# Two batches sharing the arrival of float64 weights, with clamp and gelu moved to ScalarE

## The chip, the cores and the metric

One core of one Trainium2 chip. Times are device microseconds (us) of one execution. A time given for a kernel is the median of its runs. The record marks each run as fast or slow by its granted clock and time. Engines are named as the profile has them: PE is TensorE (PEld its weight loads), DVE is VectorE, ACT is ScalarE, POOL is GpSimd, SP is SyncE, which issues the loads.

## The reference

Eight batches of 8 heads. Tokens read from 32 state vectors a head and the states read from the tokens; both results go through one gated layer whose weights are float64.

```python
B, H, S, Ns, D = 8, 8, 512, 32, 64
scores = scale * np.matmul(x, state.transpose(0, 1, 3, 2))     # softmax over states -> a
xread = np.matmul(a, state)
scores2 = scale * np.matmul(state, x.transpose(0, 1, 3, 2))    # softmax over tokens -> a2
sread = np.matmul(a2, x)
x = np.concatenate([xread, sread], axis=2)                     # ... to (B*(S+Ns), H*D)
h = x @ w_in                                                   # w_in 512 x 2048, float64
g = h * (1.0 / (1.0 + np.exp(-1.702 * h)))
return (g @ w_out).astype(np.float32)                          # w_out 2048 x 512, float64
```

## The kernel before

The weights arrive as pairs of 32-bit words, in 32 pieces of 128x512 numbers (512 KB each): 16 of `w_in`, then 16 of `w_out`. Each piece is rounded to float32 by integer and float instructions. Three raw buffers hold what has landed and isn't rounded yet.

```python
def load_weight(key, src):                     # w_in: two halves of 64 partitions; w_out: one load
    raw[key] = wpool.tile([P, 2 * FC], I32, tag="raw", ..., bufs=3)
    for i in range(src.shape[0]):
        nc.sync.dma_start(raw[key][n * i : n * (i + 1)], src[i])

def round_weight(key, dst):
    ...                                                                           # hi, lo: the words of each number
    sc = wpool.tile([P, FC], I32, tag="sc", ...)
    nc.vector.tensor_scalar(sc, hi, 0x7FF00000, None, ALU.bitwise_and)            # mask of the exponent
    nc.gpsimd.tensor_scalar(sc, sc, most, least, ALU.min, ALU.max)                # clamp
    nc.gpsimd.tensor_scalar(sc, sc, -least, 8.0, ALU.add, ALU.mult)
    nc.vector.scalar_tensor_tensor(sc, hi, -0x80000000, sc, ALU.bitwise_and, ALU.bitwise_or)
    fr = wpool.tile([P, FC], I32, tag="fr", ...)
    nc.vector.tensor_scalar(fr, hi, 0xFFFFF, 0x100000, ALU.bitwise_and, ALU.bitwise_or)
    nc.vector.scalar_tensor_tensor(dst, lo, 2.0**-32, fr, ALU.mult, ALU.add)
    nc.vector.scalar_tensor_tensor(dst, dst, 2.0**-20, sc.bitcast(FP32), ALU.mult, ALU.mult)
```

A batch's work around PE: transposes, scores and softmax; `eT`, the transposed token weights, and `sr`, the states' read with them (`srT` is its copy); `M` = states times `w_in` (four chunks); 16 "ups" (two matmuls to `h`, then gelu to `g`); 64 "downs" of `g` and `w_out` into `o`. In the kernel before, batch 0 alone does this while the weights arrive. DVE's order is left to a scheduler; the other engines run in the order of the program.

```python
def up(key, f, ntok, lhs, rhs):
    ...                                                          # matmuls into hps
    nc.scalar.activation(out=e, in_=hps, func=AF.Sigmoid, scale=1.702)
    nc.vector.tensor_tensor(out=gt, in0=hps, in1=e, op=ALU.mult)

load(0)
for c in range(NFC):                     # NFC = 4
    load_w_in(c); round_w_in(c)
    if c == 0: ...                       # all of batch 0's attention
    att_M(0, c)
load(1)
for b in range(B):
    for f in range(NF):                  # NF = 16
        if b == 0: load_w_out(f); round_w_out(f)
        up(b, f, ...)
    ...                                  # 16 groups of downs; batch b+1's attention in between
...                                      # last: ups and downs of all the states' tokens
```

## Time and profile before

| | before |
|---|---|
| median of the first three runs | 931.3 us (930.19 to 931.96) |
| PE without a gap from | 146.2 us |
| one batch from there on | 94.80 us |
| one `w_out` piece on DVE | 3.48 us |
| DVE's waits for raw weights | none |

The lines that carry this stand in the prediction. A busy row has one digit for each fortieth of the span: the busy share in tenths. A line of the timeline reads: start, duration, engine, program line, operation, out<-in, shapes, and in brackets how long the engine had been idle and what released it.

### The profile page before, as it was taken

The page shows a single profiled execution, that of the slowest core. Times are in us where ns is not written, and L with a number is a line of the kernel's source. Part 1 is how long each engine was busy: PE and PEld are TensorE (multiplying, and loading weights), DVE is VectorE, ACT ScalarE, POOL GpSimd, SP SyncE. Part 2 cuts the span into 40 slices and gives each one's busy share as a digit, 9 for nine tenths or more (in the row PEclk, how much of TensorE's full clock was granted, in tenths as well). Part 3 has the DMA queues.
Part 4 walks back from the last instruction along what each step waited for, and adds up shares of the span by engine and source line. Part 5 has one row for each costly group of instructions (what it writes and reads, how often), then busy time and mean ns, then how long its engine had stood idle before and what let it go on. Part 6 is the DMA issues. An engine that isn't in the chain of part 4 may idle for free.

```text
span 930.2 us, 7058 instructions
## 1 busy us (share of the span) xinstructions
PE 850.7 (91%) x2824; PEld 384.4 (41%) x2824; DVE 320.3 (34%) x544; ACT 169.7 (18%) x282; POOL 73.5 (8%) x104
## 2 busy tenths in 40 slices
PE   3545568999999999999999999999999999999995
PEld 1301224345444544354435443544354435444762
DVE  5786896413232223322232314231523141300110
ACT  1001111213121322122212221221222021300110
POOL 2242442000000000000000000000000000000000
PEclk8555799999999999999999999999999999999998
DMA  6256343002000200020002000200000000000001
GB/s 161 62 141 161 113 136 97 24 11 57 3 23 12 57 4 23 12 56 4 23 12 57 3 12 24 56 1 11 24 12 0 12 23 11 1 11 23 11 1 23
DMA packets 43968, 35.06 MB, mean 38 GB/s; under 512 B 37664, under 2 KB 37664, under 8 KB 43936
## 3 DMA queue, kind: packets, MB, share of 16 engines
q1 hardware_dynamic: 40832, 25.70, 10.7%
q0 software_dynamic: 3104, 8.92, 2.5%
q8 instruction: 22, 0.36, 0.2%
q14 instruction: 10, 0.08, 0.0%
HBM read 25.69 MB, written 8.91 MB: 37 GB/s over the span
## 4 chain that ended last, share of the span: by engine, by line
issue 67%; PE 18%; DVE 9%; POOL 4%; SPq 0%; DMA 0%; ACT 0%; POOLq 0%
PE o L300 11%; PE h L284 4%; POOL out_dram L306 2%; PE M L179 1%; PE sr L248 1%; DVE sc_i L133 1%; POOL sc_i L132 1%; DVE w_out L138 1%; DVE fr_o L136 1%; DVE w_out L137 1%; POOL sc_i L131 1%; DVE sc_o L133 1%; DVE w_in L138 1%; DVE g L288 1%; PE xT L169 1%
## 5 line engine op out<-in xcount | busy, mean ns | idle before, releaser
L300 PE MATMUL o<-w_out,g 128*128 128x512 f32 x1024 | 457.8, 596 | 0.0
L300 PEld LDWEIGHTS o<-w_out,g 128*128 128x128 f32 x1024 | 187.8, 190 | 236.1 <-issue 236.1
L284 PE MATMUL h<-aT,M 128*128 128x512 f32 x512 | 229.3, 606 | 21.4 <-DVE g L288 21.4
L284 PEld LDWEIGHTS h<-aT,M 128*128 128x128 f32 x512 | 92.9, 193 | 153.1 <-DVE g L288 83.4
L288 DVE TENSOR_TENSOR g<-h,e 128x512 f32<-128x512 f32 x128 | 88.4, 690 | 124.8 <-ACT e L286 124.8
L286 ACT ACTIVATE e<-h 128x512 f32<-128x512 f32 x128 | 76.4, 597 | 187.0 <-PE h L284 187.0
L179 PE MATMUL M<-w_in,stT 64*32 64x512 f32 x512 | 55.5, 658 | 26.0 <-DVE w_in L138 25.9
L306 POOL DMA_DIRECT2D out_dram<-osb x32 | 17.5, 547 | 697.7 <-ACT osb L305 697.7
L305 ACT COPY osb<-o 128x512 f32<-128x512 f32 x32 | 18.7, 586 | 192.4 <-PE o L300 192.4
L231 DVE COPY M<-M 128x512 f32<-128x512 f32 x32 | 21.8, 682 | 58.1 <-PE M L179 58.1
L231 ACT COPY M<-M 128x512 f32<-128x512 f32 x32 | 18.6, 582 | 112.6 <-PE M L179 112.6
L171 DVE COPY xT<-xT 128x512 f32<-128x512 f32 x16 | 11.1, 692 | 77.4 <-PE xT L169 77.4
L191 DVE TENSOR_REDUCE mx<-s 128x1 f32<-128x512 f32 x16 | 10.4, 687 | 79.1 <-PE s L179 79.1
L179 PEld LDWEIGHTS M<-w_in,stT 64*32 64x32 f32 x512 | 7.6, 108 | 68.1 <-issue 38.2
L248 PEld LDWEIGHTS sr<-eT,xn 128*128 128x128 f32 x256 | 33.0, 209 | 4.9 <-issue 3.3
L248 PE MATMUL sr<-eT,xn 128*128 128x64 f32 x256 | 32.9, 292 | 1.2 <-DVE eT L241 1.2
L288 DVE TENSOR_TENSOR g_sr<-h_sr,e_sr 128x256 f32<-128x256 f32 x16 | 6.8, 425 | 75.3 <-ACT e_sr L286 75.3
L257 DVE COPY srT<-sr 64x128 f32<-64x128 f32 x16 | 4.6, 289 | 73.0 <-PE sr L248 72.9
L171 ACT COPY xT<-xT 128x512 f32<-128x512 f32 x16 | 9.4, 586 | 109.6 <-PE xT L169 109.6
L284 PE MATMUL h_sr<-srT,w_in 128*128 128x256 f32 x128 | 27.8, 379 | 0.0
L300 PE MATMUL o_sr<-w_out,g_sr 128*128 128x512 f32 x64 | 27.6, 592 | 0.0
L241 DVE COPY eT<-eT 128x512 f32<-128x512 f32 x16 | 11.0, 690 | 45.5 <-PE eT L240 45.5
(52 smaller groups left out, 401.4 us busy)
## 6 DMA issues: line engine op xcount, KB each, us to landing
xn<-in_x_dram SPq DMA_DIRECT2D x64, 128.0 KB, 3.1
raw_i<-in_moe_w_in_dram SPq DMA_DIRECT2D x32, 256.0 KB, 4.2
raw_o<-in_moe_w_out_dram SPq DMA_DIRECT2D x16, 512.0 KB, 3.3
out_dram<-osb POOLq DMA_DIRECT2D x32, 256.0 KB, 2.3
stn<-in_state_dram SPq DMA_DIRECT2D x8, 64.0 KB, 2.0
out_dram<-osb_sr POOLq DMA_DIRECT2D x2, 256.0 KB, 7.1
```

Source lines behind the costliest of these rows:

```text
L133: nc.vector.scalar_tensor_tensor(sc, hi, -0x80000000, sc, ALU.bitwise_and, ALU.bitwise_or)
L138: nc.vector.scalar_tensor_tensor(dst, dst, 2.0**-20, sc.bitcast(FP32), ALU.mult, ALU.mult)
L171: (nc.scalar.copy if j % 2 else nc.vector.tensor_copy)(dst, ps.rearrange("p c q -> p (c q)"))
L179: nc.tensor.matmul(ps[g][st], A[b]["stT"][rows, st], rhs(rows, j), start=True, stop=True)
L231: (nc.scalar.copy if g else nc.vector.tensor_copy)(a["M"][:, g, FC * c : FC * (c + 1)], ps[g])
L248: nc.tensor.matmul(ps[:, j], x_heads(b, c, j), a["eT"][:, :, c, Ns * j : Ns * (j + 1)], start=(c == 0), stop=(c == SCH - 1),)
L284: nc.tensor.matmul(hps, lhs[i], rhs[i], start=(i == 0), stop=(i == n - 1))
L286: nc.scalar.activation(out=e, in_=hps, func=AF.Sigmoid, scale=1.702)
L288: nc.vector.tensor_tensor(out=gt, in0=hps, in1=e, op=ALU.mult)
L300: nc.tensor.matmul(ops, G[key][f][:, P * r : P * (r + 1)], w_out[f], start=(f == 0), stop=(f == NF - 1))
L305: nc.scalar.copy(osb, ops)
L306: nc.gpsimd.dma_start(dst, osb)
```

## The change

The intent: let batch 1's first half run on PE too while the weights arrive, so that less is left afterwards; relieve DVE of the product and of GpSimd; end the run on a plain output tile. DVE's order is now fixed by the program as well. The core of the diff:

```diff
-    ctx.enter_context(tc.manual_schedule(engines={ET.PE, ET.Activation, ET.Pool, ET.SP}))
+    ctx.enter_context(tc.manual_schedule())
@@ rounding in two parts, a and b
+    def round_a(i):
+        ...
         nc.vector.tensor_scalar(sc, hi, 0x7FF00000, None, ALU.bitwise_and)
-        nc.gpsimd.tensor_scalar(sc, sc, most, least, ALU.min, ALU.max)
-        nc.gpsimd.tensor_scalar(sc, sc, -least, 8.0, ALU.add, ALU.mult)
+        nc.scalar.activation(out=sc.bitcast(FP32), in_=sc, func=AF.Relu, bias=edge[0], scale=-8.0)
+        nc.scalar.activation(out=sc, in_=sc.bitcast(FP32), func=AF.Relu, bias=edge[1], scale=-1.0)
+    def round_b(i): ...                      # the other four DVE instructions
+    AHEAD = 2
+    def round_next(n):
+        for _ in range(n):
+            ...                              # stop behind the last piece
+            while done["a"] < min(done["b"] + 1 + AHEAD, len(PIECES)):
+                round_a(done["a"]); done["a"] += 1
+            round_b(done["b"]); done["b"] += 1
+            nxt = done["b"] + 2
+            if nxt < len(PIECES): load_weight(nxt)           # raw: bufs=3, as before
@@ gelu
-        nc.scalar.activation(out=e, in_=hps, func=AF.Sigmoid, scale=1.702)
-        nc.vector.tensor_tensor(out=gt, in0=hps, in1=e, op=ALU.mult)
+        nc.scalar.activation(out=gt, in_=hps, func=AF.Gelu_apprx_sigmoid)
@@ order of the first stage (batches 0 and 1 by chunks of M and four ups)
+    chunk(0, 0, True)                        # True: one piece is rounded after each up
+    ...                                      # batch 1's softmax
+    chunk(0, 1, True)
+    for g in range(NG): att_eT(1, g)
+    att_sread(1)
+    chunk(1, 0, False)
+    chunk(1, 1, True)
+    chunk(0, 2, True)
+    chunk(0, 3, True)
+    load_state(2); load_x(2)
+    for f in range(NF):
+        ...                                  # downs of batch 0 by rows of w_out, batch 1's other ups
+        round_next(1)
@@ the last batch
+        if not ahead: ...                    # states' ups and downs go ahead of batch 7's
```

The copies from PSUM of batches 0 and 1 all go to ScalarE, and the tile pools are resized (attention has two PSUM buffers instead of four, the downs four instead of two).

## The prediction

> **What bounds the kernel now.** I read the page first (clock and busy rows), then busy time by stretch, the chain of waits from 85 us on, the DMA issues, the timeline of the rounding stage and of the end.
>
> The busy rows say where the time is lost:
>
> ```profile
> PE   3545568999999999999999999999999999999995
> PEclk8555799999999999999999999999999999999998
> 0.00:146.22 146.22, 76.86 (x202) 27.67 (x203) 113.55 (x195) 17.65 (x28) 51.47 (x67) 0.70 0.48 133
> 146.22:931.00 784.78, 773.81 (x2624) 356.75 (x2622) 206.76 (x350) 152.09 (x254) 22.00 (x38) 0.99 0.07 20
> 290.58:385.38 94.80, 94.80 (x330) 42.30 (x329) 27.59 (x47) 20.26 (x34) 2.16 (x4) 1.00 0.08 23
> ```
>
> (columns of the last three: stretch, length, busy us and count on PE, weight loads, DVE, ACT, POOL, then clock, DMA share, GB/s). Two regimes. From 146 us the tensor engine has no gap, and a batch takes 94.80 us, so nothing but fewer matmuls or less time before that point shortens the run. Before 146 us the float64 weights arrive and are rounded to float32 piece by piece (32 pieces of 512 KB), and PE does little at a lowered clock.
>
> The chain of waits shows who paces that stage:
>
> ```profile
> 139.51 0.75 DVE fr_o L136
> 140.26 0.60 DVE g L288
> 140.85 0.60 DVE sc_o L133
> 141.46 0.60 DVE w_out L137
> 142.06 0.34 DVE sc_o L130
> 142.39 0.60 DVE w_out L138
> 142.99 0.75 DVE fr_o L136
> ```
>
> DVE is back to back, one piece in 142.99 - 139.51 = 3.48 us: five rounding instructions plus the gelu product (L288). Loads are not on this chain. Their sizes and times:
>
> ```profile
> raw_i<-in_moe_w_in_dram SPq DMA_DIRECT2D x32, 256.0 KB, 4.2
> raw_o<-in_moe_w_out_dram SPq DMA_DIRECT2D x16, 512.0 KB, 3.3
> out_dram<-osb POOLq DMA_DIRECT2D x32, 256.0 KB, 2.3
> out_dram<-osb_sr POOLq DMA_DIRECT2D x2, 256.0 KB, 7.1
> ```
>
> The last figure is us from issue to landing. They hide because a load issued when piece n is used up is first read about two pieces (7 us) later.
>
> The end: the states' output closes the run.
>
> ```profile
> 920.07 0.59 ACT L305 COPY osb_sr<-o_sr 128x512 f32<-128x512 f32 x1 [13.15 <-PE o_sr L300]
> 920.95 0.72 POOL L306 DMA_DIRECT2D out_dram<-osb_sr  x1 [13.01 <-ACT osb_sr L305]
> ```
>
> PE ends at 920.03; 920.95 + 7.1 = 928.05, and the span ends 2.1 us later.
>
> **What the Trainium skill says.** "DMA: Bandwidth & Descriptors", section "Anatomy of one DMA — SWDGE (gpsimd) path", gives a transfer a nearly constant cost of about 2 us whatever its size, most of it the receipt of the last write. The trace agrees in kind: 512 KB land in 3.3 us, so a load waited for at once cannot be cheap. "SBUF — State Buffer", section "Who interferes with whom", says that GpSimd and a DVE instruction that needs the shared port pair block each other. Before shows it: the L136 instruction takes 0.42 us alone and 0.83 us beside GpSimd, L137 0.68 and up to 1.09. "ScalarE: Activation LUTs", section "What ACT_TABLE_LOAD costs", puts a load of the tables at about 1.28 us, the same for every set; the trace has 1283 ns. "TensorE: Matmul & The Clock Gate", section "Part 1: The HAM clock gate (the "warmup" mystery)", has the array at half clock after idle windows; the clock row shows 5 tenths where PE waits.
>
> **The change part by part.**
>
> 1. Gelu as one function: takes 128 L288 products (690 ns each, 88 us) off DVE. After 146 us PE is full, so nothing is gained there. In the rounding stage it takes 0.60 us of 3.48 off each w_out piece.
>
> 2. Clamp on ScalarE: 64 GpSimd instructions go, 64 Relu activations of about 0.69 us come (the Exp with a pointer bias on 128x512 took 683 ns). DVE's slowdown beside GpSimd ends. A piece is then 0.34 + 0.34 + 0.60 + 0.60 + 0.60 = 2.5 us of DVE. If DVE alone paced it, 32 pieces would take 80 us plus two softmaxes of 10 us.
>
> 3. But the order changes. The changed order was read off the built program: the first instruction (mask of the exponent) of piece n+3 stands directly behind the last of piece n, while the load of n+3 goes into the buffer of piece n (three buffers) and waits for piece n's fourth instruction. Looking ahead two pieces with three buffers leaves no time for the load. So each step is a closed loop: mask to end of fourth instruction 0.34 + 0.34 + 0.60 + 0.68 = 1.96 us; issue 0.02; landing 3.3 us for w_out, and for w_in two halves, the second issued 0.6 us after the first and landing 3.7 us later, 4.3; start of DVE 0.05. Steps: 5.33 us (w_out), 6.33 us (w_in), against 3.5 to 3.6 now.
>
> 4. Two batches share the arrival, so PE has more to do meanwhile. Pieces that gate it, by that loop:
> - x of batch 0 and raw pieces 0 to 2 share the queue; mask of piece 2 at about 13.8 us, the x transposes' copies on ScalarE stand behind its Relus, scores end about 19.6, batch 0's softmax is done with pieces 0 and 1 rounded at 33.7.
> - pieces 2 to 7: piece 2 used up at 35.7, 3 at 42.1, then 6.33 each: piece 7 at 67.4.
> - batch 1's softmax, about 10.6 us: to 78.6. Piece 8 at 80.6, then 6.33 each: piece 13 at 112.2.
> - piece 14 needs its Relu, which stands on ScalarE behind batch 1's eT and srT copies, its M copies and five gelus; those wait for PE at half clock (sr took 7.1 us there, an up pair of matmuls 3.4 instead of 1.72). From 100 us: copies 1.2, sr 7.1, srT 0.7, M and copies 3.1, four ups 9, second M and copies 2.3, one up and its gelu 2.3: about 126. Piece 14 at 128.7, 15 at 134.1.
> - w_out, 5.33 each: piece 23 at 176.7; the mask of piece 26 at 180.1. Batch 2's x (1 MB) is queued next to that load: +1.5.
> - Batch 1's third M chunk is copied on ScalarE behind the Relus of piece 26: 1.8 + 1.2 us later, 184.5. From there PE does not wait: pieces 24 to 31 run ahead of the eight matmuls that each w_out row needs.
>
> Work of PE done by then, at full clock: attention of two batches 2 x 7.3, seven M chunks 7.2, 24 ups of 1.72 = 41.3, eight down matmuls of 0.86 = 6.9: 70 us. The whole is 8 x 94.8 + 27.5 + 27.5 = 813.4 (check: 813.4 less the 38.9 done by 146.22 is 774.5, and the trace has 920.03 - 146.22 = 773.8). Left: 743.5. With 1.5 us for the clock to come up: PE ends at 184.5 + 1.5 + 743.5 = 929.5.
>
> 5. States' tokens ahead of the last batch: the last output is a plain tile, 2.3 us to landing instead of 7.1. Tail 0.6 + 0.3 + 2.3 + 2.1 = 5.3 us instead of 10.2: gain 4.8.
>
> Sum: 929.5 + 5.3 = 934.8 by this working. The terms I padded (half clock through all of batch 1's chunk, the contention of batch 2's x) rather err high, so I say 932: the sharing gains 31 us of PE work, the slower arrival costs 40, the tail gives back 5.
>
> **Rivals.** (a) The loads don't bind: DVE paces at 2.5 us a piece, all pieces rounded near 110 us, PE full from about 85. PE left then about 765: 860 us or so, 7% faster. For it: every instruction cost of the new step is lower. Against: the order and the wait of the load are fixed in the program, and DVE takes its instructions in order. (b) ScalarE as the bound in the shared stage: per step a gelu 0.6 and two Relus 1.4 = 2.0 us, below 5.3, so no, except where a Relu stands behind PE work (piece 14, counted). If other Relus are caught so, another 10 us: 945. (c) The steady stage gets a new wait, from two attention buffers in PSUM instead of four, and the fourth M chunk inside the ups. Copies take 0.6 to 0.7 us and four down matmuls (3.4 us) lie between users, so I expect none; 1 us a batch would make 7 us. (d) Landing is shorter when only one piece is in flight: w_out already had one in flight in before and took 3.3, so little; 0.5 us a step would give 11 us: 921.
>
> **Range and chances.** The loop has 20 or so load steps on the path; 0.3 us each is 6 us, the ScalarE hold-up of piece 14 is uncertain by 6, the start by 3, the rest by 4: together 10 us, widened for an error of structure: 914 to 948. Faster by over 2% means under 912.7 and needs the loads to be half hidden: 0.14. Slower means over 950: 0.08. Within 2%: 0.78.
>
> **What would show it.** Right: DVE waits for the raw loads nearly every piece, about 2.8 us for w_out and 3.7 for w_in, some 90 us in all; masks of successive w_out pieces 5.3 us apart; PE full only from about 185 us with batches of 94.8 after; no idle on POOL's account; span end about 5 us after the last matmul. Wrong: w_out pieces at 2.5 to 3.5 us, PE full before 150 us (then rival a), or gaps in PE after 200 us (rival c).

## More of the kernel before

One more view is needed later, PE's waits in the first 240 us of the kernel before (engine, line, what it waited for: us in total, times, longest):

```profile
PE M L179 <- DVE w_in L138: 25.9, 11, 4.5
PE h L284 <- DVE g L288: 21.4, 10, 9.3
```

PE waits for rounded `w_in` pieces, and its ups wait for the gelu product, which DVE does between the rounding of `w_out`.

## The result, and the profile after

The changed kernel took 946.51 us (946.0 to 948.57, 4 runs) against 931.19 us (930.19 to 931.96, 4 runs) of the kernel before: ratio 1.0169, 95% interval 1.0151 to 1.0187. A ratio is the mean time of one kernel's fast runs over that of the other's fast runs of the same rounds, so not quite the ratio of the medians. It is 1.7% slower, which is within 2%. The profiled execution took 944.6 us.

The page of the changed kernel, busy rows and clock:

```profile
PE   2555384689999999999999999999999999999997
PEclk9786587889999999999999999999999999999999
DVE  1737424444014001500050005000500050000000
```

PE is now below nine tenths for nine slices of 23.6 us instead of seven of 23.3, and DVE, busy five to nine tenths in the first seven slices before, is busy four tenths at most from the fifth slice to the tenth: DVE's work no longer paces this stage. Busy time by stretch (columns as in the prediction):

```profile
0.00:192.39 192.39, 98.37 (x371) 44.86 (x371) 88.38 (x165) 75.90 (x124) 0.77 (x8) 0.79 0.36 90
253.30:348.10 94.80, 94.80 (x330) 42.95 (x329) 16.12 (x28) 21.77 (x36) 4.46 (x8) 1.00 0.11 34
```

The second line shows only that PE is never idle in the steady stage; a stretch of that length need not be one batch. The outputs of successive batches show its length:

```profile
289.72 0.54 POOL L364 DMA_DIRECT2D out_dram<-osb  x1 [15.33 <-ACT osb L363]
384.87 0.54 POOL L364 DMA_DIRECT2D out_dram<-osb  x1 [15.33 <-ACT osb L363]
```

A batch takes 95.15 us; before, the same outputs lie 94.80 us apart (290.04 and 384.84). PE does not wait in it, so these 0.35 us are longer work of PE, and no run tells why; over five batches they make 1.7 us. The rest of the loss lies ahead of 192.39 us, where PE's last long gap ends (it was 146.22). DVE's waits in the first 240 us:

```profile
DVE sc L147 <- DMA raw_i<-in_moe_w_in_dram: 58.8, 13, 7.2
DVE sc L147 <- DMA raw_o<-in_moe_w_out_dram: 45.7, 16, 3.7
DVE sc L159 <- ACT sc L149: 7.9, 1, 7.9
```

104.5 us for raw weights, where there were none. The timeline of DVE over one `w_in` piece and the next mask, and over two `w_out` masks, shows the loop:

```profile
107.37 0.43 DVE L147 TENSOR_SCALAR sc<-raw_i 128x512 int32<-128x512 int32 x1 [4.27 <-DMA raw_i<-in_moe_w_in_dram]
107.72 0.42 DVE L158 TENSOR_SCALAR fr<-raw_i 128x512 int32<-128x512 int32 x1
108.05 0.68 DVE L159 SCALAR_TENSOR_TENSOR sc<-raw_i,sc 128x512 int32<-128x512 int32 x1
108.66 0.68 DVE L160 SCALAR_TENSOR_TENSOR w_in<-raw_i,fr 128x512 f32<-128x512 uint32 x1
109.37 0.69 DVE L161 SCALAR_TENSOR_TENSOR w_in<-w_in,sc 128x512 f32<-128x512 f32 x1
114.29 0.43 DVE L147 TENSOR_SCALAR sc<-raw_i 128x512 int32<-128x512 int32 x1 [4.22 <-DMA raw_i<-in_moe_w_in_dram]
...
145.39 0.43 DVE L147 TENSOR_SCALAR sc<-raw_o 128x512 int32<-128x512 int32 x1 [2.67 <-DMA raw_o<-in_moe_w_out_dram]
150.85 0.43 DVE L147 TENSOR_SCALAR sc<-raw_o 128x512 int32<-128x512 int32 x1 [2.75 <-DMA raw_o<-in_moe_w_out_dram]
```

L147 at 107.37 masks the piece two ahead; L158 to L161 finish the current one. L160 is the last reader of the raw buffer, so the next load is issued at 109.4, lands just before 114.3, and its mask is the very next instruction in DVE's order. The step is 114.29 - 107.37 = 6.92 us for `w_in` and 150.85 - 145.39 = 5.46 us for `w_out`, of which DVE works about 2.7. (The `w_out` steps after 140 us range from 5.1 to 6.4, with a median of 5.4. Before, the steps were 3.5 to 3.6 us.)

The third wait, 7.9 us, is on ScalarE. Its queue around that time, and the DVE instruction concerned:

```profile
107.83 0.72 ACT L148 ACTIVATE sc<-sc,edge 128x512 f32<-128x512 int32 x1 [5.00 <-DVE sc L147]
108.59 0.72 ACT L149 ACTIVATE sc<-sc,edge 128x512 int32<-128x512 f32 x1
109.22 1.05 ACT L286 COPY eT<-eT 128x512 f32<-128x512 f32 x2
117.45 0.53 ACT L302 COPY srT<-sr 64x128 f32<-64x128 f32 x2 [7.18 <-PE sr L293]
120.06 1.07 ACT L276 COPY M<-M 128x512 f32<-128x512 f32 x2 [2.08 <-PE M L214]
...
133.84 0.71 ACT L148 ACTIVATE sc<-sc,edge 128x512 f32<-128x512 int32 x1
```

```profile
135.34 0.69 DVE L159 SCALAR_TENSOR_TENSOR sc<-raw_i,sc 128x512 int32<-128x512 int32 x1 [7.92 <-ACT sc L149]
```

The queue is crossed both ways. Batch 1's `eT` copies stand behind the Relus of piece 13 (L148, L149), whose mask waits for a load; the Relus of piece 14 (133.84) stand behind batch 1's copies and gelus, which wait for PE. The Trainium skill, "PSUM — Partial Sum Buffer", section "Engine vs sequencer instructions", says that ScalarE's, VectorE's and GpSimd's queues are strict FIFO; these lines agree: the copy that was ready on PE since about 92.5 us ran at 109.22, directly behind the Relus.

What PE lost by it, its two largest waits in the first 240 us:

```profile
PE h L333 <- ACT M L276: 35.0, 8, 13.1
PE sr L293 <- ACT eT L286: 18.5, 2, 17.8
```

Further down PE's list stand 8.1 and 6.0 us for the first `stT` and `xT` copies, also on ScalarE behind Relus; before, PE waited for no copy there. They stay with four buffers (7.9 and 6.1 us in experiment 12). No run moved copies back to VectorE, so what these waits cost is not known.

The end of the run is as intended, a plain tile, from whose issue to the end of the span it is 4.6 us:

```profile
939.16 0.58 ACT L363 COPY osb<-o 128x512 f32<-128x512 f32 x1 [13.15 <-PE o L358]
940.04 0.54 POOL L364 DMA_DIRECT2D out_dram<-osb  x1 [13.19 <-ACT osb L363]
```

PE ended at about 939.1, the span at 944.6: a tail of 5.5 us instead of 10.2.

### The profile page after: what moved, and what is told of

It reads as the page before. It is cut to its first block, busy times and chain, and to the rows that moved or that the text cites. A ratio compares the mean times of both kernels' runs of the same rounds, so it can differ in the third digit from the quotient of the medians.

```text
span 944.6 us, 6837 instructions
## 1 busy us (share of the span) xinstructions
PE 844.3 (89%) x2824; PEld 392.2 (42%) x2824; DVE 203.1 (22%) x366; ACT 229.1 (24%) x380; POOL 19.7 (2%) x42
## 4 chain that ended last, share of the span: by engine, by line
issue 66%; PE 15%; DMA 8%; DVE 6%; POOL 2%; SPq 1%; ACT 1%; POOLq 0%; DVEq 0%; ACTq 0%
PE o L358 10%; DMA raw_i<-in_moe_w_in_dram 4%; DMA raw_o<-in_moe_w_out_dram 4%; PE h L333 3%; POOL out_dram L364 2%; DVE sc L159 1%; DVE sc L147 1%; PE M L214 1%; DVE w_in L160 1%; PE sr L293 1%; SPq L122 1%; DVE fr L158 1%; SPq L102 1%; DVE w_out L160 1%; PE xT L206 0%
## 5 line engine op out<-in xcount | busy, mean ns | idle before, releaser
L333 PE MATMUL h<-aT,M 128*128 128x512 f32 x512 | 233.6, 612 | 35.0 <-ACT M L276 35.0
L333 PEld LDWEIGHTS h<-aT,M 128*128 128x128 f32 x512 | 98.9, 196 | 169.4 <-issue 115.0
L335 ACT ACTIVATE g<-h 128x512 f32<-128x512 f32 x128 | 76.1, 595 | 141.1 <-PE h L333 141.1
L214 PE MATMUL M<-w_in,stT 64*32 64x512 f32 x512 | 45.0, 622 | 16.4 <-DVE w_in L161 16.4
L276 DVE COPY M<-M 128x512 f32<-128x512 f32 x24 | 16.4, 682 | 194.6 <-PE M L214 194.6
L293 PE MATMUL sr<-eT,xn 128*128 128x64 f32 x256 | 33.0, 292 | 18.5 <-ACT eT L286 18.5
L148 ACT ACTIVATE sc<-sc,edge 128x512 f32<-128x512 int32 x32 | 23.0, 720 | 81.3 <-DVE sc L147 81.2
L206 PE MATMUL xT<-ident,xn 128*128 128x128 f32 x128 | 22.9, 310 | 21.9 <-ACT stT L199 8.1
L206 PEld LDWEIGHTS xT<-ident,xn 128*128 128x128 f32 x128 | 18.2, 161 | 36.5 <-issue 14.6
L333 PEld LDWEIGHTS h_sr<-srT,w_in 128*128 128x128 f32 x128 | 24.3, 190 | 3.7 <-issue 0.5
L149 ACT ACTIVATE sc<-sc,edge 128x512 int32<-128x512 f32 x32 | 23.1, 722 | 1.1
```

Source lines behind the costliest of these rows:

```text
L148: nc.scalar.activation(out=sc.bitcast(FP32), in_=sc, func=AF.Relu, bias=edge[0], scale=-8.0)
L149: nc.scalar.activation(out=sc, in_=sc.bitcast(FP32), func=AF.Relu, bias=edge[1], scale=-1.0)
L206: nc.tensor.transpose(ps[:, c], x_heads(b, c, j), ident)
L214: nc.tensor.matmul(ps[g][st], A[b]["stT"][rows, st], rhs(rows, j), start=True, stop=True)
L276: copies(b, g)(m[:, g], ps[g])
L293: nc.tensor.matmul(ps[:, j], x_heads(b, c, j), a["eT"][:, :, c, Ns * j : Ns * (j + 1)], start=(c == 0), stop=(c == SCH - 1),)
```

## The experiments

Theory: with three raw buffers and a mask that looks two pieces ahead in a fixed order, the load stands in a closed loop with DVE; this, and not any of the other parts, takes back what the sharing gains. Rivals: the order of ScalarE's queue is the main cost; or one of the other parts (clamp on ScalarE, gelu, states ahead) costs time. All twelve kernels gave correct results; each was compared with runs of the kernel before on the same chip.

**1. Look ahead by one piece.** The changed kernel with

```diff
-    AHEAD = 2
+    AHEAD = 1
```

> The changed kernel with the look-ahead of the masks cut from two pieces to one, nothing else. Theory (the closed loop of mask, last read, load, mask costs the time): the load of a piece now has one whole piece of DVE work more to land in, so DVE's waits for the raw loads fall from 104.5 us to under 40 us, w_out pieces follow each other in about 2.7 us instead of 5.4 and w_in pieces in about 3.5 instead of 6.9, PE is without gaps from about 120 us instead of 192, and the run takes about 875 us (860 to 890). Rival (ScalarE's order and PE's half clock bind the shared stage, the loads only fill slack): the waits move to ScalarE and the run stays above 920 us.

Measured: 900.14 us (899.12 to 901.5), ratio to before 0.9667 [0.9652, 0.9682]. One digit turns 1.7% slower into 3.3% faster. The direction was right; 900 is above the expected range. Its DVE waits say why:

```profile
DVE sc L159 <- ACT sc L149: 34.3, 7, 20.7
DVE sc L147 <- DMA raw_i<-in_moe_w_in_dram: 19.6, 6, 7.0
...
DVE sc L147 <- DMA raw_o<-in_moe_w_out_dram: 6.8, 5, 4.3
```

The waits for weights fell from 104.5 to 26.4 us, but the wait for Relus rose from 7.9 to 34.3: with the loads mostly out of the way, ScalarE's queue was the next in line. (A look-ahead of one also leaves each Relu one piece less time; this run can't part the two.)

**2. A fourth raw buffer.** The changed kernel, look-ahead kept at two:

```diff
-        raw[i] = wpool.tile(..., bufs=3)
+        raw[i] = wpool.tile(..., bufs=4)
-            nxt = done["b"] + 2
+            nxt = done["b"] + 3
+    load_weight(3)                           # after load_x(1)
```

> The changed kernel with four raw buffers instead of three and each load issued one piece earlier, the look-ahead of the masks kept at two. Theory (the load has no time because buffers and look-ahead leave none): same effect as the run with the look-ahead of one, 860 to 890 us and within 1% of it. Rival (it is the position of the mask that costs, through ScalarE's queue, not the missing buffer): clearly slower than the run with look-ahead one, above 900 us.

Measured: 891.45 us (889.35 to 893.12), ratio 0.9569 [0.9553, 0.9585]: 55 us less than the changed kernel. Just above the range, and 1.0% below the first experiment, at the edge of the 1% that was expected. DVE waited 28.8 us for weights and 20.9 us for Relus; `w_out` pieces followed each other in 2.73 us. Two different ways to open the loop gave nearly the same, which is what the theory says and neither rival does.

**3. States ahead alone.** The kernel before, with the states' ups and downs moved ahead of batch 7's downs.

```diff
+        if b == B - 1:
+            for f in range(NF): up("sr", f, ...)
+            ...                              # and their downs
-    for f in range(NF): up("sr", f, ...)     # no longer at the end
```

> The kernel before with the states' tokens moved ahead of the last batch, nothing else. Theory: the last output lands in 2.3 us instead of 7.1, so 4.8 us less, about 926.4 us, with PE's busy span unchanged. Rival: the span's end is not set by that landing; then no change within 0.2%.

Measured: 926.28 us (925.85 to 927.36), ratio 0.9947 [0.9935, 0.9959]. As expected; this part gains about 5 us.

**4. The gelu function alone.** The kernel before with the one ScalarE function in place of sigmoid and product.

```diff
-        nc.scalar.activation(out=e, in_=hps, func=AF.Sigmoid, scale=1.702)
-        nc.vector.tensor_tensor(out=gt, in0=hps, in1=e, op=ALU.mult)
+        nc.scalar.activation(out=gt, in_=hps, func=AF.Gelu_apprx_sigmoid)
```

> The kernel before with gelu as one ScalarE function, nothing else. Theory (DVE paces the w_out pieces, 3.48 us each with the 0.60 us product in it): 16 pieces lose 0.6 us each, PE is full about 9.6 us earlier, about 921.5 us. Rival (the step is set by DVE and GpSimd blocking each other, not by the count of DVE instructions): under 3 us gained.

Measured: 918.25 us (917.92 to 918.46), ratio 0.9857 [0.9844, 0.9871]; 3 us better than expected. PE's timeline of this kernel:

```profile
89.96 28.95 PE L283 MATMUL h<-aT,M 128*128 128x512 f32 x64
```

All 16 ups run in one go. The 21.4 us of waits for the product, shown above for the kernel before, are gone, and 9.3 us of waits of the downs for `w_out` pieces have come: 12 us net. The DVE step itself hardly moved (10.1 us for three pieces, 3.37 each, instead of 3.48): in two of three pieces an instruction that takes 0.68 us alone took 1.09, as beside GpSimd. The gain is a wait removed, not a step shortened.

**5. The clamp alone.** The kernel before with the two Relus in place of GpSimd's clamp.

```diff
-        nc.gpsimd.tensor_scalar(...)         # two
+        nc.scalar.activation(..., func=AF.Relu, bias=edge[0], scale=-8.0)
+        nc.scalar.activation(..., func=AF.Relu, bias=edge[1], scale=-1.0)
```

> The kernel before with the clamp alone moved to ScalarE (two Relu activations a piece), DVE's order left to the scheduler, sigmoid and product kept. Theory: DVE is no longer held by GpSimd, so a w_in step shrinks from about 3.6 to 2.5 us and a w_out step (with the product) from 3.48 to about 3.1; 16 x 1.1 + 16 x 0.4 = 24 us at most, less what loads of 4.3 us no longer hide: 905 to 920. Rival: the Relus stand in ScalarE's queue behind copies and sigmoids and DVE waits for them, so the time stays within 5 us of 931 or rises.

Measured: 923.52 us (921.06 to 925.34), ratio 0.9922 [0.99, 0.9944]: a gain of 7 us, where at least 11 was expected. DVE's timeline, two `w_in` pieces:

```profile
69.02 0.69 DVE L139 SCALAR_TENSOR_TENSOR sc_i<-raw_i,sc_i 128x512 int32<-128x512 int32 x1 [0.48 <-ACT sc_i L138]
...
72.32 0.69 DVE L139 SCALAR_TENSOR_TENSOR sc_i<-raw_i,sc_i 128x512 int32<-128x512 int32 x1 [0.48 <-ACT sc_i L138]
```

A `w_in` step is 3.30 us, not 2.5: the scheduler starts the mask of a piece only after the piece before is finished, and the two Relus (1.4 us) are longer than the two instructions it puts between, so DVE waits for them. The `w_out` step was 3.08 us, as expected (3.1).

**6. The whole change but the sharing and its order.** The kernel before with the edits of 3, 4 and 5, DVE left to the scheduler.

> The kernel before with the clamp on ScalarE, the gelu function and the states ahead, that is the change without the sharing of the arrival and without its fixed order. Theory (the fixed order costs more than the sharing gains): the three parts together are worth about 5 + 13 + some 10 to 20, so 893 to 905, some 45 us below the changed kernel. Rival (the sharing is roughly neutral, the other parts are what eats the gain): 930 to 950.

Measured: 910.93 us (908.66 to 911.09), ratio 0.9781 [0.9762, 0.9801]. A little above the range (the clamp gave less), far from the rival. So the three other parts gain 20 us together, and the sharing in its order, with the copies on ScalarE and the resized pools, costs 36 (946.5 - 910.9). With the same three raw buffers, this kernel's DVE waits for weights come to 2.4 us:

```profile
DVE sc_i L135 <- DMA raw_i<-in_moe_w_in_dram: 1.5, 1, 1.5
DVE sc_o L135 <- DMA raw_o<-in_moe_w_out_dram: 0.9, 3, 0.5
```

Three buffers are enough in one order of DVE and not in the other.

**7. One Relu early.** The changed kernel with the mask and Relus of piece 14 put ahead of batch 1's transposes:

```diff
     chunk(0, 1, True)
+    round_a(done["a"]); done["a"] += 1
     for g in range(NG): att_eT(1, g)
```

> The changed kernel with the mask and the two Relus of piece 14 issued before batch 1's transposes, so that they don't stand behind its copies on ScalarE; DVE's own order is unchanged. Theory: the 7.9 us wait of DVE for that Relu goes and about 2 us come back at piece 15, so 938 to 942. Rival (the hold-up hides behind PE's own work of batch 1, so it costs nothing): 945 to 948. If all 13.5 us of the hold-up came off: 933.

Measured: 950.0 us (947.92 to 950.71), ratio 1.0205 [1.0188, 1.0221]. Slower than the changed kernel; both the theory and its rival missed. ScalarE's queue, then DVE's:

```profile
113.93 0.72 ACT L148 ACTIVATE sc<-sc,edge 128x512 f32<-128x512 int32 x1 [5.42 <-DVE sc L147]
114.69 0.72 ACT L149 ACTIVATE sc<-sc,edge 128x512 int32<-128x512 f32 x1
115.31 1.05 ACT L286 COPY eT<-eT 128x512 f32<-128x512 f32 x2
```

```profile
144.31 0.69 DVE L159 SCALAR_TENSOR_TENSOR sc<-raw_i,sc 128x512 int32<-128x512 int32 x1 [12.37 <-ACT sc L149]
```

I had looked at one direction of the crossing only. The Relu taken forward waits for a mask, and the mask for a load; the `eT` copy behind it now ran at 115.31 instead of 109.22, all of batch 1 slid by six us, and the next Relu, of piece 15, waited 12.4 us instead.

**8. Four buffers, two Relus early, batch 1's state read later.** The second experiment with `round_a` of pieces 14 and 15 ahead of batch 1's chunks and the `eT` transposes and state read behind its chunk 1.

```diff
     chunk(0, 1, True)
+    for _ in range(2): round_a(done["a"]); done["a"] += 1     # sc with bufs=4, fr with bufs=1
+    chunk(1, 0, False)
+    chunk(1, 1, True)
     for g in range(NG): att_eT(1, g)
     att_sread(1)
-    chunk(1, 0, False)
-    chunk(1, 1, True)
```

> The changed kernel with four raw buffers (as in the second experiment, 891.45 us), masks and Relus of pieces 14 and 15 early, and batch 1's eT transposes and state read behind its first two chunks instead of ahead of them. In the second experiment TensorE waited 7.2 us for the eT copy, then read the states at half clock in 7.1 us, and only then began batch 1's chunks at 89 us; the 17.5 us wait of DVE on ScalarE was covered by those chunks. Theory: chunks start about 11 us earlier and the read costs 3.5 us later at full clock: 876 to 886. Rival (pieces, not the order of TensorE's work, set the time from there): within 4 us of 891.

Measured: 899.16 us (898.02 to 900.26), ratio 0.9662 [0.9646, 0.9678], 8 us worse than the second experiment. The same mistake: the M copies of batch 1 stood behind the Relus taken forward, whose masks waited 1.5 and 2.3 us for their loads, and PE waited 12.7 us for those copies at 88.29.

**9. Four buffers, new order.** From 7 and 8: neither Relus ahead of copies nor copies ahead of Relus, but work that needs no new piece first, and the pieces between ups that follow at once.

```diff
     chunk(0, 0, True)
+    att_M(0, 1)
     ...                                      # batch 1's softmax
-    chunk(0, 1, True)
-    (eT transposes and state read of batch 1)
-    chunk(1, 0, False)
+    chunk(0, 1, False, m=False)              # M is there already
+    chunk(1, 0, True)
     chunk(1, 1, True)
     chunk(0, 2, True)
     chunk(0, 3, True)
+    (eT transposes and state read of batch 1)
```

> The second experiment (four raw buffers, 891.45 us) with batch 1's work in another order, so that ScalarE's queue is no longer crossed both ways: the M of chunk 1 ahead of batch 1's softmax, chunk 1 of batch 0 without rounding, then batch 1's chunks 0 and 1 with four pieces each between their ups, and batch 1's eT transposes and state read behind the last chunk of batch 0. Theory: no copy of batch 1 stands behind a Relu that waits for a load, and no Relu behind a copy that waits for TensorE; TensorE ends the four chunks at about 92 us instead of 110 and reads the states later at full clock (5 us): 874 to 884. Rival (TensorE is starved by the pieces all the same): within 5 us of 891. If it is above 896, the reading of ScalarE's queue is wrong again.

Measured: 884.6 us (884.36 to 885.6), ratio 0.9505 [0.9492, 0.9518]. Just above the theory's range of 874 to 884, outside the rival's; the four chunks ended at about 91 us.

**10. The same order with three buffers.** The changed kernel with the edit of 9 alone.

> The changed kernel with the order of the run before and nothing else: three raw buffers and the mask two pieces ahead stay. Theory: the load loop of 6.9 and 5.4 us a piece still sets the pace, only the hold-up of piece 14 (13.5 us from piece 13 to 14, where a plain step is 6.9) goes: 946.5 - 6.6 = 940, so 937 to 943. Rival (the order is the main cost, the loads hide): under 925. If piece 14's hold-up only moves again, as with the early Relu: 946 or more.

Measured: 946.64 us (946.52 to 947.39), ratio 1.017 [1.0157, 1.0184]: to 0.1 us the changed kernel. The order gained 7 us with four buffers and nothing with three. DVE's wait for Relus had shrunk to 1.2 us and the rounding ran 8 us ahead (the mask of piece 17 at 132.07 us; 140.03 in the changed kernel). PE lost it again:

```profile
178.10 7.09 PE L293 MATMUL sr<-eT,xn 128*128 128x64 f32 x32 [12.01 <-ACT eT L286]
```

The `eT` copies, now behind other Relus, waited for other loads.

**11 and 12. The state read last.** Both orders again, with the `eT` transposes after the 13th group of batch 0's downs and the state read after the 15th, when no Relu is left.

```diff
     chunk(0, 3, True)
-    (eT transposes and state read of batch 1)
     ...
     for f in range(NF):
         ...
+        if f == 12: (eT transposes of batch 1)
+        if f == 14: (state read of batch 1)
```

Three buffers:

> The run of the changed kernel in the new order (946.64 us) with batch 1's eT transposes and state read moved again, to the end of batch 0's down matmuls, when no Relu is left on ScalarE. There the rounding was 8 us ahead of the changed kernel's, but TensorE waited 12.0 us for the eT copies (behind Relus that wait for loads) and read the states at half clock in 7.1 us. Theory: the 20 us from the end of the transposes to the first down matmul go and 4.6 us come back later at full clock, hidden behind nothing: 946.6 - 15.5 = 931, so 927 to 935. If the loads alone set the end (the downs then wait for pieces instead): 940 or more.

Measured: 942.53 us (941.8 to 943.08), ratio 1.013 [1.0117, 1.0144]: 4 us gained of 15.5 expected. The rival's number came true, but not its form: no down waits for a piece in PE's list. The wait for `eT` copies was gone (0.7 us), and the waits for M copies rose to 52.1 us; the last of them is

```profile
183.67 3.69 PE L333 MATMUL h<-aT,M 128*128 128x512 f32 x4 [10.67 <-ACT M L276]
```

again a copy behind Relus that wait for loads: the loads set the end through ScalarE's queue. Add PE's two waits on ScalarE's copies (M and `eT`), in us: changed kernel 35.0 + 18.5 = 53.5; experiment 10 39.9 + 12.7 = 52.6; experiment 11 52.1 + 0.7 = 52.8; experiment 7 30.9 + 25.9 = 56.8. In these four kernels with the slow loop the sum hardly changes, and order only chooses whose copy pays. With four buffers it was 14.9 + 7.9 = 22.8 in the second experiment.

Four buffers:

> The fastest version so far (four buffers, new order, 884.6 us) with the same move of the eT transposes and state read. There the wait was 2.5 us, the read 6.0 us instead of 3.5, and the downs after it began at a lowered clock (8.2 us instead of 7.0). Theory: 2.5 + 2.5 + 1.2 = 6 us off: 877 to 881. Rival (a wait for the first w_out pieces or for M copies takes their place): 883 to 887.

Measured: 878.5 us (five runs, 878.25 to 883.82), ratio 0.9456 [0.9433, 0.9479], as expected. One of the five runs took 883.82 us; why stays open. This version beats both kernels, by 5.4% and by 7.2% (878.5 / 946.5 = 0.928). Its page:

```profile
PE   2678799999999999999999999999999999999997
PEclk9799999999999999999999999999999999999999
```

PE's waits for the M and `eT` copies are 13.1 + 0.7 us, its last gap ends at 159.6 us (0.7 us), and the first above nine tenths is the sixth slice of 22 us. Against experiment 6, which has all but the sharing, this is 32.4 us less by the medians, 30 by the ratios (0.9781 - 0.9456). That is the sharing together with its fixed order of DVE, its copies on ScalarE and the fourth buffer; the sharing by itself was not measured.

## Why the prediction was right or wrong

It was right in the verdict (within 2%) and in the mechanism, and the measured 946.5 lies in its range of 914 to 948, but 14.5 us above the predicted 932 and near the edge; one of the four runs, 948.57, lies outside.

| step of the prediction | predicted | measured in the profiled run |
|---|---|---|
| batch 0's softmax done | 33.7 | 38.05 |
| a `w_in` step | 6.33 | 6.92 |
| piece 13 used up | 112.2 | 123.2 |
| piece 14 used up (hold-up by ScalarE) | 128.7 (16.5) | 136.6 (13.5) |
| a `w_out` step | 5.33 | 5.4 (median; 5.1 to 6.4) |
| mask of piece 26 | 180.1 | 189.9 |
| last long gap of PE ends | 184.5 | 192.4 |
| a batch after it | 94.8 | 95.15 |
| last matmul ends | 929.5 | 939.1 |
| tail | 5.3 | 5.5 |
| DVE's waits for raw weights | some 90 | 104.5 |
| end | 934.8, said 932 | 944.6 |

- **The closed loop (part 3)** is shown: experiments 1 and 2 open it in two ways and take 46 and 55 us off, and experiment 6 has the buffers without the loop and 2.4 us of waits. The term that was mis-sized is the landing of a `w_in` piece. I took 4.3 us from the first half's issue, giving the second half a landing of 3.7 us; the second half, issued about half a us after the first, took 4.3 us by itself (the chain of waits has a 4.31 us transfer there, and the median of all halves is 4.2; a whole `w_out` piece lands in 3.3, and no run tells why the half is slower). That is 0.59 us a step in ten steps (pieces 3 to 7 and 9 to 13), 5.9 us. The section that the prediction cites for a nearly constant cost, "Anatomy of one DMA — SWDGE (gpsimd) path" in "DMA: Bandwidth & Descriptors" of the Trainium skill, is about transfers issued from GpSimd; these loads are issued from SyncE, so the agreement is in kind only.
- **The start (part 4)** was 4.3 us short: batch 0's softmax was done at 38.05 us. The mask of piece 2 came at 17.39 us, after a wait for its load, where the working has 13.8: that is 3.6 of the 4.3.
- **The hold-up of piece 14** was mis-sized by 3 us in the other direction. 4.3 + 5.9 - 3.0 is 7.2 of the 7.9 us by which piece 14 came late, and the last gap ends 7.9 us late too, as said: behind the copy of batch 1's third M chunk (191.77 us). That the hold-up took back 3 us is luck. (The sum has a slip as well: 67.4 + 10.6 is 78.0, not 78.6.)
- **The step that failed** is the last one, from 934.8 to 932: "rather err high" was an unmeasured feeling about two terms, and the terms that erred were others, and low. The working as it stood missed by 10 us of 945, the stated figure by 12.6 of the profiled run. The working's 934.8 is also a span, and the time of a run is 1.7 to 1.8 us longer (946.34 against 944.6), which was left out.
- **Gelu and tail (parts 1 and 5).** The tail is as said (experiment 3). Gelu was given 0.6 us on each `w_out` piece of DVE; alone it gains 13 us (experiment 4), through PE's ups that no longer wait. Within the change neither is part of the loop, and no run took gelu out of it.
- **Clamp (part 2).** 2.5 us of DVE work a piece is about right: a `w_out` step under four buffers was 2.73. Left to the scheduler it's 3.30 on `w_in`, for the order's sake (experiment 5).
- **The sharing gains 31 us of PE work.** At the end of its last gap PE had 773.8 us to go before and 746.7 in the changed kernel (939.1 - 192.4), 27 us less. The working has 743.5 + 1.5 = 745.0; the 1.7 us between are about what the longer batches make. Experiments 6 and 12 differ by 30 to 32 us, but in more than the sharing, so they only fit it.
- **Rivals.** (a) fell: the loads bind. (b) is what the queue shows once at piece 14, counted; no other Relu held DVE in the changed kernel. That Relus hold PE's copies stands in part 4 at two places (the x transposes, the third M chunk), but I hadn't summed it: PE waited 53.5 us for `eT` and M copies. (c) fell as a wait: there is a single one of 0.7 us after 200 us, though a batch takes 95.15 us instead of 94.80. (d) fell: 5.4 us a step, no shorter landing.

## What to carry to other kernels

When a program fixes the order of an engine, count the buffers against the look-ahead: with three buffers, a first instruction two pieces ahead stands directly behind the instructions that free the buffer for its load, and each step then costs a whole landing. One more buffer, or one piece less of look-ahead, was worth 55 and 46 us here, more than the 27 us of PE work that the sharing moved. A queue that serves both a load-fed stream and PE's copies couples the two, so ask of each entry what the entry ahead of it waits for, in both directions; moving one entry only moved the wait until the loop itself was open. And when a prediction's own sum is at hand, don't shave it by feel.

## What the Trainium skill lacked or had wrong

- "ScalarE: Activation LUTs", section "What ACT_TABLE_LOAD costs", adds a drain of about 1.38 us to a load of 1.28, 2.66 us in all for a switch. In the second experiment the load starts as the Relu before it ends (57.96 + 0.72 = 58.68) and is followed by the next function at once, so this switch cost 1.3 us:

```profile
57.96 0.72 ACT L149 ACTIVATE sc<-sc,edge 128x512 int32<-128x512 f32 x1
58.70 1.28 ACT L234 ACT_TABLE_LOAD   x1
60.00 0.69 ACT L234 ACTIVATE e<-s,mx 128x512 f32<-128x512 f32 x1
```

- "PSUM — Partial Sum Buffer" has ScalarE's queue as strict FIFO, and the runs agree, but no page that I read says what it costs when such a queue mixes entries fed by loads with entries fed by PE: 53 to 57 us of PE's waits in four orders of this kernel with three buffers, 14 to 29 us in four orders with four.
- "SBUF — State Buffer", section "Who interferes with whom", is not wrong in saying that DVE and GpSimd block each other; what it lacks is how little that can be worth. Taking GpSimd out of the rounding alone gained 7 us of 931 (experiment 5): DVE waited 7.7 us for the two Relus that took its place, where it had waited 6.2 us for GpSimd's results before.
